# Delta attention and two MoE layers on one core: MoE from chunk 0's first tokens, packed diagonal blocks, VectorE transposes, another order of weight loads

## The chip, the cores and the metric

One core of a Trainium2 chip runs the whole program. Its engines are TensorE (PE, with its weight loads PEld), VectorE (DVE), ScalarE (ACT), GpSimd (POOL) and SyncE (SP, which issues most transfers); each works through its own instructions in order and waits on semaphores of the others. The metric is the device time of one execution in microseconds (us).

## The reference

```python
B, H, S, D = 4, 8, 768, 48                      # float32
k_n = k / (norm(k) + 1e-6); state = zeros((B, H, D, D))
for t in range(S):
    y[:, :, t] = q_t @ state                    # per head
    v_old = state^T @ k_n_t
    state = state + beta_t * outer(k_n_t, v_t - v_old)
x = y.transpose(0, 2, 1, 3).reshape(3072, 384)
x = maximum(x @ w_in, 0) ** 2 @ w_out           # d_ff 2048, weights float64
g = x @ w_gate
out = (g * sigmoid(g) * (x @ w_val)) @ w_out2   # d_ff 1536, weights float64
```

## The kernel before

The sequence is cut into six chunks J of 128 steps, each in two halves c of 64. With all four batches a chunk gives 512 tokens (TOK; HT is 256, the tokens of one c). Of the 32 pairs of batch and head, p picks 16 partitions' worth of heads, and each tile of 128 partitions holds two blocks of 64.

For a chunk, attention solves a triangular system per head: the Gram blocks of the keys (`gram`, `gram0`), masked and scaled by beta, are inverted and merged into NT. Chunk 0 inverts 16x16 blocks on DVE (`invert16`) and merges them twice on PE: `d_merge1` and `d_merge2` to 32x32, `tr11`, `merge1`, `merge2` to 64x64. The other chunks send their masked Gram (`m_out`) to memory, load it in another layout (`t_load`), invert 32x32 blocks on POOL (`invert`), and fetch the result (`n_out`, `n_back`). Then per half c come the correction by the state (`ks`), the solution u (`uu`), the output y (`y0` for chunk 0, straight into MoE's input xh and xl; `yy` for the others, through memory, `fetch_x` and `split_x`) and the state (`do_ku`). c=1 needs the state of c=0.

The first MoE layer runs chunk by chunk over 16 steps m of 128 hidden features: `moe1_h` (nine matmuls to ps_h), ACT's Relu and squares, DVE's low part hl, `moe1_o` (nine into ps_y, held in PSUM over all m). Products are split in a high and a low fp32r part. HMS[J] says how many of the first m run on half the tokens, c by c. The weights are float64 words of 16 pieces of 768 columns, w_in and w_out in turn, two m each. `Piece` turns a piece into its two parts: ACT's Abs into f, three DVE operations (lines 180, 182, 187), ACT's high part (200), and the low part (203) on DVE or POOL, as `conv_lo` says. The converted pieces are then kept for all chunks. The second MoE layer follows at the end and is not touched.

The order on DVE, ACT, POOL, PE and SP is that of the code where `manual_schedule` names the engine. Ahead of the MoE loop it is written out by hand (lines 1124 to 1227). In the loop, a list `first` (and `plan` for later chunks) gives a time slot to each attention stage: a full m step is two slots, a half one is one. `conv_slot` and `need` bring the conversions along. Chunk J+1's MoE waits for its x. In the kernel before, all of chunk 0's attention stands ahead of the first MoE matmul, and the list starts with chunk 1's scores.

Of the kernel before, what the change touches and what calls it, by code (L numbers as in the profile page):

```python
# [21 lines left out]
def delta_attention_moe_moe2_kernel(  # L22
# [186 lines left out]
    raw1 = {  # L209
        (pc, kd): wp.tile([128, Z * PIECE], WDT, tag="w", name="raw")  # L210
        for pc in range(NP1 - 2) for kd in range(2)
    }
# [255 lines left out]
    def m0(J, c, p):
        m, ps = MS[J, c, p], g0.pop((J, c, p))
        for d, r in parts(p):  # L470
            nc.vector.scalar_tensor_tensor(out=m[d], in0=ps[r], scalar=-1.0, in1=m[d], op0=ALU.mult, op1=ALU.mult)


# [204 lines left out]
    def tr11(J, c):  # L678
        ts = [
            TD[0][:, p] if J == 0 and c else ap.tile([128, 8, 32], F32, tag="tq", bufs=2, name="tq") for p in range(2)  # L680
        ]
        if J == 0:
            pss = banks([128, 8, 32], "ps_tq")
            for h in range(8):
                for p in range(2):
                    for b0 in (0, 64):
                        nc.tensor.matmul(
# [716 lines left out]
```

## Time and profile before

| what | us |
|---|---|
| median of 3 runs (1082.63 to 1083.14) | 1083.07 |
| the profiled execution, its own time | 1081.49 |
| its span, first to last instruction | 1079.6 |
| PE busy | 995.8 (92%) |
| DVE busy | 610.7 (57%) |
| ACT busy | 398.4 (37%) |
| POOL busy | 249.5 (23%) |

The shares are means over stages with different limits, so they are read by stretches. In the page's 40 slices of 27 us PE has 3, 3, 6, 7, 6, 7, 8 and 8 tenths in the first eight and 9 in nearly all others; DVE has 6 to 8 there.

### The profile page before, as it was taken

To read this page: it belongs to the slowest core of one execution; us is meant where nothing else is said; L and a number is where in the kernel's file an instruction comes from. 1 tells how busy PE (TensorE), PEld (TensorE's weight loads), DVE (VectorE), ACT (ScalarE), POOL (GpSimd) and SP (SyncE) were. 2 spreads that over 40 slices of the span, in tenths; PEclk is the share of its full clock that TensorE was granted. 3 is DMA by queue.
4 is the path that set the end of the run, shared out by engine and by line. 5 is a ranking of instruction groups with operands and counts; after the bars stand their busy time and mean duration, and the time that the engine had idled before them with its cause. 6 is when DMAs were issued, how large, how long until landed. Compare 5 with 4: busy or idle time off the path is not lost.

```text
span 1079.6 us, 24471 instructions
## 1 busy us (share of the span) xinstructions
PE 995.8 (92%) x10591; PEld 816.5 (76%) x10591; DVE 610.7 (57%) x979; ACT 398.4 (37%) x765; POOL 249.5 (23%) x373
## 2 busy tenths in 40 slices
PE   3367678899999999999999999999999999999998
PEld 3355556688887787787788878888888888888886
DVE  6647888778567667754546995343343343433333
ACT  6243545542353344344347873132231222312222
POOL 3629417914811940950000000000000000000000
PEclk9998888989999999999999999999999999999999
DMA  9474044526235253231015660010010100100000
GB/s 301 174 195 126 2 104 109 138 77 149 66 101 122 68 132 73 59 99 42 20 30 197 193 240 13 1 59 1 1 59 1 53 7 1 59 1 1 30 0 30
DMA packets 118267, 84.51 MB, mean 78 GB/s; under 512 B 91664, under 2 KB 95632, under 8 KB 118160
## 3 DMA queue, kind: packets, MB, share of 16 engines
q1 hardware_dynamic: 116960, 77.97, 26.1%
q0 software_dynamic: 1056, 4.72, 1.1%
q8 instruction: 83, 1.36, 0.5%
q10 hardware_dynamic: 144, 0.26, 0.1%
q14 instruction: 24, 0.20, 0.1%
HBM read 61.70 MB, written 21.23 MB: 77 GB/s over the span
## 4 chain that ended last, share of the span: by engine, by line
PE 68%; issue 9%; DMA 5%; DVE 4%; ACT 2%; POOL 1%; SPq 1%; ACTq 0%; DVEq 0%; POOLq 0%
PE ps_o L1083 14%; PE ps_v L1058 13%; PE ps_g L1058 13%; PE ps_h L957 11%; PE ps_y L991 11%; DMA raw<-in_moe_w_gate_dram 1%; PE ps_y L784 1%; DVE raw L182 1%; PE ps_k L732 1%; PE ps_g L431 1%; DVE w L203 1%; PE ps_u L747 1%; PE ps_a L541 1%; DMA x2raw<-y_scr 1%; DMA y_scr<-ye 1%
## 5 line engine op out<-in xcount | busy, mean ns | idle before, releaser
L957 PE MATMUL ps_h<-xh,w 128*128 128x512 f32 (+1 forms) x636 | 206.8, 385 | 12.9 <-DVE w L203 12.8
L991 PE MATMUL ps_y<-hh,w 128*128 128x512 f32 (+1 forms) x606 | 157.4, 394 | 10.0 <-DVE w L203 4.7
L957 PEld LDWEIGHTS ps_h<-xh,w 128*128 128x128 f32 x636 | 119.0, 193 | 37.5 <-DVE w L203 14.6
L1062 DVE SCALAR_TENSOR_TENSOR th<-th,ps_g 128x512 f32<-128x512 f32 x72 | 49.5, 687 | 170.6 <-ACT th L1061 170.5
L1058 PE MATMUL ps_g<-x2h,w 128*128 128x512 f32 x432 | 144.8, 389 | 0.0
L1058 PE MATMUL ps_v<-x2h,w 128*128 128x512 f32 x432 | 144.7, 389 | 0.0
L960 ACT ACTIVATE r<-ps_h 128x512 f32<-128x512 f32 (+1 forms) x106 | 58.9, 556 | 218.2 <-PE ps_h L957 213.9
L991 PEld LDWEIGHTS ps_y<-hh,w 128*128 128x128 f32 x606 | 109.6, 192 | 33.0 <-DVE w L203 5.6
L957 PE MATMUL ps_h<-xl,w 128*128 128x512 f32 (+1 forms) x318 | 120.1, 378 | 0.0
L590 POOL TENSOR_TENSOR TMP<-T 128x30 f32<-128x30 f32 (+9 forms) x150 | 92.2, 615 | 111.7 <-DMA T<-m_scr 69.0
L1083 PE MATMUL ps_o<-ph,w 128*128 128x512 f32 x432 | 111.9, 389 | 1.4 <-ACT ye L1007 1.4
L1061 ACT ACTIVATE th<-ps_g 128x512 f32<-128x512 f32 x72 | 43.1, 599 | 180.2 <-PE ps_g L1058 180.2
L597 POOL TENSOR_TENSOR T<-T,TMP 128x30 f32<-128x30 f32 (+9 forms) x150 | 95.2, 635 | 11.0
L1083 PEld LDWEIGHTS ps_o<-ph,w 128*128 128x128 f32 x432 | 81.0, 188 | 18.6 <-ACT ye L1007 1.9
L1065 ACT ACTIVATE ph<-th 128x512 fp32r<-128x512 f32 x72 | 45.4, 631 | 133.1 <-DVE th L1063 133.1
L1058 PEld LDWEIGHTS ps_g<-x2h,w 128*128 128x128 f32 x432 | 81.1, 188 | 17.1 <-issue 0.3
L1058 PEld LDWEIGHTS ps_v<-x2h,w 128*128 128x128 f32 x432 | 81.1, 188 | 16.8
L991 PE MATMUL ps_y<-hl,w 128*128 128x512 f32 (+1 forms) x303 | 84.0, 386 | 1.5 <-DVE hl L977 1.5
L976 DVE TENSOR_TENSOR r<-r 128x512 f32<-128x512 f32 (+1 forms) x72 | 50.2, 697 | 62.0 <-ACT hh L961 61.5
L1058 PE MATMUL ps_v<-x2l,w 128*128 128x512 f32 x216 | 84.0, 389 | 0.0
L1058 PE MATMUL ps_g<-x2l,w 128*128 128x512 f32 x216 | 84.0, 389 | 0.0
L977 DVE TENSOR_TENSOR hl<-r,hh 128x512 fp32r<-128x512 f32 (+1 forms) x106 | 74.6, 705 | 12.7 <-ACT r L964 8.0
(137 smaller groups left out, 1384.2 us busy)
## 6 DMA issues: line engine op xcount, KB each, us to landing
raw<-in_moe_w_out_dram SPq DMA_DIRECT2D x13, 768.0 KB, 5.2
raw<-in_moe_w_in_dram SPq DMA_DIRECT2D x8, 768.0 KB, 11.4
KT<-in_kt_dram SPq DMA_DIRECT2D x12, 448.0 KB, 6.4
m_scr<-M SPq DMA_DIRECT2D x20, 256.0 KB, 2.4
KB<-in_kn_dram SPq DMA_DIRECT2D x12, 384.0 KB, 6.0
AQ<-in_q_dram SPq DMA_DIRECT2D x24, 192.0 KB, 4.9
V<-in_v_dram SPq DMA_DIRECT2D x12, 384.0 KB, 3.9
raw<-in_moe_w_gate_dram SPq DMA_DIRECT2D x6, 768.0 KB, 4.4
```

The source lines that it names most:

```text
L590: eng.tensor_tensor(tmp[:, r0:r1], t_[:, r0:r1, kk:kk + 1].to_broadcast([n, r1 - r0, w]), t_[:, kk:kk + 1, kk + 1:].to_broadcast([n, r1 - ...
L597: eng.tensor_tensor(t_[:, r0:r1, kk + 1:], t_[:, r0:r1, kk + 1:], tmp[:, r0:r1], op=ALU.add)
L957: nc.tensor.matmul(ps, w_[:, kk], x_[:, kk, cols], start=n == 0, stop=n == 3 * KD - 1)
L960: nc.scalar.activation(out=r, in_=ps, func=ACTF.Relu)
L976: nc.vector.tensor_tensor(r, r, r, op=ALU.mult)
L977: nc.vector.tensor_tensor(hl, r, hh.bitcast(F32), op=ALU.subtract)
L991: nc.tensor.matmul(acc[f], w_[:, fs], h_, start=first, stop=m == NM1 - 1 and n == 2)
L1058: nc.tensor.matmul(ps, w_[:, kk], x_[:, kk], start=n == 0, stop=n == 3 * KD - 1)
L1061: nc.scalar.activation(out=th, in_=gp, func=ACTF.Tanh, scale=0.5)
L1062: nc.vector.scalar_tensor_tensor(out=th, in0=th, scalar=1.0, in1=gp, op0=ALU.add, op1=ALU.mult)
L1065: nc.scalar.activation(out=hh, in_=th, func=ACTF.Copy)
L1083: nc.tensor.matmul(o_acc[J][f], w_[:, fs], h_, start=m == 0 and n == 0, stop=m == NM2 - 1 and n == 2)
```

## The change

Ahead of the loop, chunk 0's diagonal 32x32 blocks go from PSUM into a packed tile DG (`g_diag`) before they are transposed, all 128 partitions in one transpose; the other Gram blocks follow (`g_off`). Chunk 1's Gram is copied by ACT (`m_copy`) and masked and scaled by POOL (`m_mask`, `m_beta`). `tr11` transposes on DVE instead of by matmuls with the identity. The scores of chunk 0's c=1 and of chunk 1 are copied by ACT and masked by POOL instead of masked by DVE. Only the first half of chunk 0 is finished ahead of the loop; the c=1 half's stages move into `first`. HMS goes to 6 for chunk 0 and 2 for chunk 1, chunk 2's slots four later. Three weight pieces are asked for at the start, the others one by one between other transfers. The first two low parts go to POOL.

```diff
-    HMS = [0, 1, 1, 1, 1, 1]
-    LAGS = [0] * 6
+    HMS = [6, 2, 1, 1, 1, 1]
+    LAGS = [0, 0, 4, 0, 0, 0]
...
-                if turn[0] and not last_in:
+                if turn[0] and not last_in and not held:
...
-    conv_lo = [nc.vector]
+    conv_lo = [nc.gpsimd]
...
+    def g_diag(c, p):
+        ps = g0[0, c, p]
+        for b0 in range(0, 128, 32):
+            r0, f0 = ps_row(p, b0), b0 % 64
+            out_, in_ = DG[b0:b0 + 32, 16 * c + 8 * p:16 * c + 8 * p + 8], ps[r0:r0 + 32, :, f0:f0 + 32]
+            if p == 0:
+                copy(out_, in_)
+            else:
+                nc.vector.tensor_copy(out_, in_)
...
+    def m_copy(J, c, p):
...
+        for d, r in parts(p):
+            nc.scalar.activation(out=m[d], in_=ps[r], func=ACTF.Copy, scale=-1.0)
+
+    def m_mask(J, c, p):
+        m = MS[J, c, p]
+        nc.gpsimd.tensor_tensor(m, m, mask.unsqueeze(1).to_broadcast([128, 8, 64]), op=ALU.mult)
...
-        nc.gpsimd.tensor_tensor(BM, BM, bT.unsqueeze(1).to_broadcast([128, 32, 32]), op=ALU.mult)
+        nc.vector.tensor_tensor(T, T, bT.unsqueeze(1).to_broadcast([128, 32, 32]), op=ALU.mult)
...
-        for b0 in range(0, 128, 32):
-            f0 = b0 % 64
-            nc.vector.transpose(
-                out=T[b0:b0 + 32], in_=NTT[b0:b0 + 32, :, f0:f0 + 32].rearrange("s x t -> s t x")
-            )
+        nc.vector.transpose(out=T, in_=DG.rearrange("s x t -> s t x"))
...
-                            ident[b0:b0 + 32, b0:b0 + 32], start=True, stop=True,
...
+            src = NT[c][p][:, :, 0:32] if J else ND[:, 16 * c + 8 * p:16 * c + 8 * p + 8]
+            nc.vector.transpose(out=t11[c, p], in_=src)
...
-    for pc, kd in ((1, 0), (1, 1), (2, 0), (2, 1), (3, 0), (3, 1), (4, 0)):
-        load_w1(pc, kd)
...
+    load_w1(1, 0)
+    make_identity(nc, ident)
...
+    stage("y", 0, 0)
     run_all(("tload", 1, c) for c in P2)
     run(("v", 1, 0))
     run(("mback", 1, 0))
     run(("ku", 0, 0))
+    held.clear()
+    merge16("d1", 1)
+    run(("vn", 0, 1))
+    conv(2)
+    flush()
+    run(("inv", 1, 0, 1, nc.gpsimd))
...
-            8: [("gram", 2, 0)],
-            10: [("gram", 2, 1), ("loadw", 7, 0)],
-            13: [("nout", 1), ("nback", 1, 0), ("nback", 1, 1), ("vn", 1, 1)],
...
+            0: [("d2", 1, 0), ("d2", 1, 1)],
+            0.5: [("ks", 0, 1)],
+            1: [("t11", 0, 1), ("m1", 0, 1), ("dcopy", 1)],
...
+            15: [("gram", 2, 1), ("loadw", 7, 0)],
...
+            16.5: [("nout", 1), ("nback", 1, 0), ("tload", 2, 0), ("tload", 2, 1), ("nback", 1, 1)],
```

PE around chunk 0's u of c=0. ps_d and ps_e are the merges to 32x32, ps_tq the transposes by identity, ps_m and ps_x the merges to 64x64, ps_u is u, ps_y is y, ps_s the state. Before:

```order
L653 MATMUL ps_d<-own,ND 32x16 x64
L687 MATMUL ps_tq<-own,ND 32x32 x32
L671 MATMUL ps_e<-ND,own 32x16 x64
L704 MATMUL ps_m<-tq,NT 32x32 x32
L687 MATMUL ps_tq<-own,ND 32x32 x32
L719 MATMUL ps_x<-ND,tq 32x32 x32
L747 MATMUL ps_u<-V,NT 64x48 x32
L704 MATMUL ps_m<-ND,NT 32x32 x32
```

Now, from the first merge of c=0 on:

```order
L665 MATMUL ps_d<-NDT,ND 32x16 x64
L683 MATMUL ps_e<-ND 32x16 x64
L701 MATMUL ps_m<-tq,NT 32x32 x32
L716 MATMUL ps_x<-ND,tq 32x32 x32
L744 MATMUL ps_u<-V,NT 64x48 x32
L814 MATMUL ps_y<-AQ_100,RS_103 32x64 x32
L814 MATMUL ps_y<-AQ_100,RS_104 32x64 x32
```

The second half's merges (ps_d, ps_tq, ps_e of c=1) stood between c=0's steps; now u of c=0 follows its own merges, and y comes directly behind it.

DVE behind the scaling of that u (RS is the tile of u and the state). f and raw rows are conversion steps, xl the low part of MoE's input, hl that of a MoE block, V the correction of c=1 by the state. Before:

```order
L753 TENSOR_TENSOR RS0_103<-ps_u_972,bB_98 64x8x48 x2
L753 TENSOR_TENSOR RS1_104<-ps_u_973,bB_98 64x8x48 x2
L560 TENSOR_TENSOR AQ1_101<-ps_a_1132,mask_96 64x512 x2
L560 TENSOR_TENSOR AQ1_101<-ps_a_1133,mask_96 64x512 x2
L740 TENSOR_TENSOR V_163<-V_163,ps_k_1239 128x384
L740 TENSOR_TENSOR V_163<-V_163,ps_k_1240 64x384 x2
L203 TENSOR_TENSOR w1_827<-raw_116,w1_827 128x6x128
L187 SCALAR_TENSOR_TENSOR raw_117<-raw_117 128x768
```

Now:

```order
L834 TENSOR_TENSOR xl_868<-ps_y_833,xh_867 128x3x64
L834 TENSOR_TENSOR xl_868<-ps_y_834,xh_867 128x3x64
L834 TENSOR_TENSOR xl_868<-ps_y_873,xh_867 128x3x64
L834 TENSOR_TENSOR xl_868<-ps_y_874,xh_867 128x3x64
L179 TENSOR_SCALAR f_831<-f_831 128x768
L181 SCALAR_TENSOR_TENSOR raw_157<-raw_157,f_831 128x768
L974 TENSOR_TENSOR hl_1104<-r_1102,hh_1103 128x256
L974 TENSOR_TENSOR hl_1121<-r_1119,hh_1120 128x256
L737 TENSOR_TENSOR V_155<-V_155,ps_k_1218 128x384
L737 TENSOR_TENSOR V_155<-V_155,ps_k_1219 64x384 x2
L186 SCALAR_TENSOR_TENSOR raw_157<-raw_157 128x768
L202 TENSOR_TENSOR w1_1256<-raw_157,w1_1256 128x6x128
```

The low parts hl of the first two half blocks and the conversion steps now stand ahead of c=1's correction, which before had come first.

SP from the first values on. V are values, raw weight pieces, M the masked Gram of chunk 1 on its way out and T its way back, AQ, KB and KT the next queries and keys. Before:

```order
L325 DMA V_163<-in_v_dram 128x768
L141 DMA raw_118<-in_moe_w_in_dram 128x3x512
L141 DMA raw_119<-in_moe_w_out_dram 128x2x768
L141 DMA raw_120<-in_moe_w_in_dram 128x3x512
L141 DMA raw_121<-in_moe_w_out_dram 128x2x768
L141 DMA raw_122<-in_moe_w_in_dram 128x3x512
L141 DMA raw_123<-in_moe_w_out_dram 128x2x768
L141 DMA raw_124<-in_moe_w_in_dram 128x3x512
L527 DMA m_scr1_90<-M_712 128x8x64
L527 DMA m_scr1_90<-M_714 128x8x64
L527 DMA m_scr1_90<-M_874 128x8x64
```

Now:

```order
L321 DMA V_155<-in_v_dram 128x768
L139 DMA raw_157<-in_moe_w_in_dram 128x3x512
L539 DMA m_scr1_90<-M_442 128x8x64
L539 DMA m_scr1_90<-M_444 128x8x64
L539 DMA m_scr1_90<-M_451 128x8x64
L539 DMA m_scr1_90<-M_453 128x8x64
L544 DMA T_109<-m_scr1_90 32x32x32 x4
L321 DMA V_915<-in_v_dram 128x768
L642 DMA NT_102<-m_scr1_90 32x16x32 x2
L139 DMA raw_1090<-in_moe_w_out_dram 128x2x768
L139 DMA raw_1092<-in_moe_w_in_dram 128x3x512
L317 DMA AQ0_100<-in_q_dram 48x2x512 x2
```

Nine pieces were asked for ahead of the stores of M; now three are, and the fourth comes behind the stores, the loads of T and chunk 1's values.

## Rows read from the trace of the kernel before

**Rows 1.** Stage table of core 0: busy us (instructions) per engine, granted clock, DMA share, GB/s.

```profile
0.00:87.00 87.00, 42.16 (x1854) 38.40 (x1856) 53.55 (x126) 35.34 (x127) 41.64 (x58) 0.98 0.72 214
87.00:150.00 63.00, 42.14 (x457) 31.25 (x446) 47.95 (x69) 25.57 (x39) 32.32 (x46) 0.81 0.21 59
150.00:219.00 69.00, 59.94 (x1006) 47.37 (x1005) 58.54 (x81) 39.05 (x72) 49.50 (x67) 0.92 0.51 126
219.00:630.00 411.00, 407.44 (x5340) 332.61 (x5339) 272.81 (x457) 184.48 (x350) 123.93 (x199) 1.00 0.38 101
630.00:1080.00 450.00, 444.10 (x1956) 366.83 (x1956) 177.82 (x251) 113.92 (x178) 2.15 (x4) 1.00 0.08 27
```

**Rows 2.** Timeline of DVE: start us, us, operation, count, idle before and releaser.

```profile
14.44 7.79 DVE L487 STREAM_TRANSPOSE T<-NT 32x1024 f32<-32x1024 f32 x4
...
33.71 1.88 DVE L494 STREAM_TRANSPOSE own<-T 128x1024 f32<-128x1024 f32 x1
...
71.62 2.81 DVE L560 TENSOR_TENSOR AQ<-ps_a,mask 64x512 f32<-64x512 f32 x4 [9.12 <-PE ps_a L541]
```

**Rows 3.** Timeline of ACT, start of the program.

```profile
13.06 2.40 ACT L567 ACTIVATE AQ<-ps_a 64x512 f32<-64x512 f32 x4 [0.89 <-PE ps_a L541]
...
36.84 0.37 ACT L655 ACTIVATE ND<-ps_d,lower 128x128 f32<-128x128 f32 x1 [10.03 <-PE ps_d L653]
...
47.20 1.54 ACT L676 ACTIVATE tq<-ps_tq 32x256 f32<-32x256 f32 x4 [2.19 <-PE ps_tq L687]
```

**Rows 4.** Timeline of PE: one stop, and the first MoE matmul.

```profile
39.38 1.51 PE L671 MATMUL ps_e<-ND 32*32 32x16 f32 x98 [1.33 <-issue]
...
87.14 0.50 PE L957 MATMUL ps_h<-xh,w 128*128 128x512 f32 x1
```

**Rows 5.** Groups by line and shape, 0 to 220 us: count | busy us, mean ns | idle.

```profile
L187 DVE SCALAR_TENSOR_TENSOR raw<-raw 128x768 int32<-128x768 int32 x15 | 18.2, 1210 | 0.2
...
L182 DVE SCALAR_TENSOR_TENSOR raw<-raw,f 128x768 int32<-128x768 int32 x15 | 16.2, 1078 | 0.4
...
L203 DVE TENSOR_TENSOR w<-raw,w 128x768 fp32r<-128x768 f32 x11 | 13.2, 1201 | 0.1
L977 DVE TENSOR_TENSOR hl<-r,hh 128x512 fp32r<-128x512 f32 x15 | 13.0, 869 | 2.8 <-ACT r L964 2.8
...
L560 DVE TENSOR_TENSOR AQ<-ps_a,mask 64x512 f32<-64x512 f32 x16 | 11.0, 688 | 12.1 <-PE ps_a L541 11.8
...
L180 DVE TENSOR_SCALAR f<-f 128x768 int32<-128x768 int32 x15 | 10.6, 705 | 17.1 <-ACT f L174 16.9
...
L203 POOL TENSOR_TENSOR w<-raw,w 128x768 fp32r<-128x768 f32 x4 | 8.3, 2065 | 35.9 <-ACT w L200 35.9
...
L370 ACT ACTIVATE junk<-KB 128x48 f32<-128x48 f32 x32 | 7.2, 229 | 3.0 <-DMA KB<-in_kn_dram 3.0
```

**Rows 6.** Timeline of SP's DMA issues from 150 us.

```profile
150.07 0.36 SPq L527 DMA_DIRECT2D m_scr<-M  x1
...
151.40 0.43 SPq L624 DMA_DIRECT2D n_scr<-T  x1
...
161.56 2.62 SPq L532 DMA_DIRECT2D T<-m_scr  x4
...
218.17 0.33 SPq L624 DMA_DIRECT2D n_scr<-T  x1
```

**Rows 7.** Timeline of POOL: first and last operation of chunk 2's inverse.

```profile
168.92 0.25 POOL L590 TENSOR_TENSOR TMP<-T 128x30 f32<-128x30 f32 x1 [5.90 <-DMA T<-m_scr]
...
217.91 0.24 POOL L597 TENSOR_TENSOR T<-T,TMP 128x30 f32<-128x30 f32 x1
```

**Rows 8.** Chain of work that ended last, 222 to 232 us: start us, us, what.

```profile
223.46 1.07 PE ps_h L957 x9
...
225.61 2.07 PE ps_h L957 x9
...
230.82 0.68 PE ps_m L704 x50
```

More of the change, by code (lines that the diff above doesn't have):

```diff
@@ L150, in delta_attention_moe_moe2_kernel @@
     last_in = []
+    held = [1]
     class Piece:
@@ L208, in delta_attention_moe_moe2_kernel @@
     LAST = (NP1 - 1, 1)
[L209 to L212, printed above, removed]
+    raw1 = {}
     conv1 = [(pc, kd, 0) for pc in range(NP1) for kd in range(2)] + [(*LAST, 1)]
@@ L468, in m0, with ps_row @@
[L468 to L471, printed above, removed]
+    def ps_row(p, b0):
+        return (b0 + 64 * p) % 128
+    def g_diag(c, p):
[7 more added lines that the diff above has]
+                nc.vector.tensor_copy(out_, in_)
@@ new lines, in g_off @@
+    def g_off(c, p):
+        ps = g0.pop((0, c, p))
+        for b0 in (0, 64):
+            r0 = ps_row(p, b0)
+            nc.scalar.activation(
+                out=NT[c][p][b0:b0 + 32, :, 32:64], in_=ps[r0:r0 + 32, :, 32:64], func=ACTF.Copy, scale=-1.0
+            )
+    def m_copy(J, c, p):
+        if J == 1 and c:
+            m = ap.tile([128, PIECE], F32, tag="xf", bufs=2, name="M")[:, 0:512].rearrange("q (h t) -> q h t", h=8)
+        else:
+            m = ap.tile([128, 8, 64], F32, tag="xr", bufs=XR, name="M")
+        MS[J, c, p], ps = m, g0.pop((J, c, p))
+        for d, r in parts(p):
+            nc.scalar.activation(out=m[d], in_=ps[r], func=ACTF.Copy, scale=-1.0)
@@ L678, in tr11 @@
     def tr11(J, c):
[L679 to L687, printed above, removed]
[L688 to L697 removed]
+        for p in range(2):
+            t11[c, p] = ap.tile([128, 8, 32], F32, tag="tq", bufs=2, name="tq")
+            src = NT[c][p][:, :, 0:32] if J else ND[:, 16 * c + 8 * p:16 * c + 8 * p + 8]
+            nc.vector.transpose(out=t11[c, p], in_=src)
     def merge1(J, c):
@@ L1122, in merge16 @@
         run_all((w, c, p) for p in P2)
-    run_all(("kt", 0, c) for c in P2)
-    nc.sync.dma_start(out=bB, in_=beta)
-    run_all(("kb", 0, c) for c in P2)
-    nc.gpsimd.memset(BM, 1.0)
+    nc.gpsimd.memset(NTT, 0.0)
+    nc.gpsimd.memset(BM, -1.0)
     nc.gpsimd.affine_select(
@@ L1148, in delta_attention_moe_moe2_kernel @@
         )
-    make_identity(nc, ident)
     for p in P2:
@@ L1158, in delta_attention_moe_moe2_kernel @@
     run(("brows",))
-    run(("din",))
-    run(("amm", 0, 0))
     run_all(("gram0", 1, c) for c in P2)
+    for c in P2:
+        run_all(("go", c, p) for p in P2)
+    run(("sums", 1, 0))
+    run_all(("amm", 0, c) for c in P2)
+    stage("mcopy", 1, 0)
+    run(("sq", 1, 1, 0))
+    stage("mcopy", 1, 1)
     run(("acopy", 0))
-    run_all(("sums", 1, c) for c in P2)
-    run(("root", 1, None, 0))
+    run(("acopy", 1))
     ahead()
@@ L1297, in delta_attention_moe_moe2_kernel @@
                 load_last()
-            conv_lo[0] = nc.gpsimd if n in range(5, 8) else nc.vector
+            if n and J and not seq[n - 1][0]:
+                order.close()
+                order.enter_context(tc.manual_schedule(engines={mybir.EngineType.DVE, mybir.EngineType.Activation}))
             nxt = seq[n + 1] if n + 1 < len(seq) else None
```

186 lines of the change are left out of this document (81 added, 105 removed).

## The prediction

> **What bounds the kernel now.** I read the stage table first [rows 1]. From 219 us on, TensorE (PE) is busy all but 9.5 us of 861, at full clock; nothing the change does can shorten that part except by starting it earlier. [...] So the question is when the kernel gets to that dense part. The first MoE matmul stands at 87.14 [rows 4]. From there to 219 VectorE (DVE) is the busiest: 47.95 of 63 and 58.54 of 69 us. It turns each float64 weight piece into fp32r parts by four operations, 0.71 + 1.08 + 1.21 + 1.20 = 4.2 us [rows 5], seventeen times, and its idle times are waits for PE or ScalarE (ACT), such as the 9.12 us ahead of 71.62 [rows 2].
>
> A second chain runs through the queue of SyncE (SP) and GpSimd (POOL). The last masked Gram block of chunk 2 leaves for memory at 150.07, queued ahead of chunk 1's inverse (issued 151.40); then chunk 2's blocks come back (loads from 161.56), POOL inverts them from 168.92 to 218.15, and the result leaves at 218.17 [rows 6, 7]. PE uses it at 230.82 [rows 8]. I call the 150.07 T: chunk 1's merge and chunk 2's inverse both hang on it. From T to 230.82 are 80.7 us.
>
> **The front, step by step.** The diagonal blocks were transposed 32 partitions at a time, 7.79 us [rows 2]; packed in DG they need one transpose of the size of line 494, 1.88. The packing is eight 32x256 copies on DVE, a form it does not show; ACT's takes 0.385 (1.54 for four) and DVE's 64x512 mask 0.688 [rows 3, 5]; I take 0.40, by ACT's row of the same shape. With 5 us for the norms' root, now behind the transpose, and the 13.4 us that run from the end of line 487 to the end of line 494, NDT is ready at about 6.9 + 3.2 + 1.9 + 5 + 1.4 (the new multiply by beta, 1024 columns at the mask's rate) + 13.4 = 31.8 instead of 35.6.
>
> ACT is level with that. Ahead of the first merge copies its order now holds eight copies (3.1), sixteen sums (half of the 7.2 for 32), six Gram copies (3.6 at 0.60 [rows 3]), eight score copies (4.8) and three operations of 384 to 768 columns (1.8): 16.9 us after a root at about 15.8, so 32.7, when PE's first product, a microsecond behind NDT, is there too; before, these copies started at 36.84, so 4 us are won. Should ACT's order run late, the chain runs late with it, since nothing hides it. From there: copies and second merge of c=0 to 37.3 (one stop of PE within, below), the two transposes of 128x256 (a quarter of 1.88, 0.47 each) to 38.3, first merge product 39.2, ACT held by an Abs until 40.4 and copying to 41.9, second product, a high part and four copies to 44.4, u to 45.6, its DVE scaling to 47.8. The transposing PE products (two blocks of 32), chunk 0's c=1 merge and its second state are no longer ahead of MoE. y, the state and c=1's first merge are 160 products in one go. PE stops for 1.33 us ahead of 39.38 with no releaser but "issue", and does so after every 128 of the small matmul records [rows 4]; I allow two stops of 2 us beside 3 us of work. First MoE matmul: about **55**, 32 us earlier. If the packing copies cost 0.69, 2 us later; without the stops, 4 earlier.
>
> [...]
>
> **How much of the 32 us lasts.** MoE now runs six m steps on 256 tokens, with weights as they come, then the same six on the other half. A half block costs PE 1.07 against 2.07 us [rows 8], so halving is nearly free. But the pieces come at DVE's pace, so I count DVE's work up to T, in the new order. Before: 53.55 + 47.95 = 101.5 us busy of 150 [rows 1], 48.5 idle. Taken away: transposes 5.9, two Gram copies (at 0.69) 1.4, twelve score masks 8.3 (chunk 0's c=1 and chunk 1 now go ACT and POOL), six Gram masks 4.1, three subtractions that fall behind T 1.6; together 21.3. Added: packing 3.2, beta 1.4, more conversion steps 9.1 (3 x 0.71 + 2 x 1.08 + 3 x 1.21 + 1.20; two low parts go to POOL), two sums 1.0, two copies 1.2, four transposes 1.9, and twelve half-width low parts for three full ones, 12 x 0.47 - 3 x 0.87 = 3.0 (0.47: a little over half of 0.87); together 20.8. So DVE has **101.0** us to do before T, as before: T moves only by the idle time that the order fills. Waits that I can name there: the first Gram 7, ACT's root 1.5, u 2, the first y 3, the first two half blocks 5, the correction by the state 3, u, y and state of c=1 7: 28.5. I add 10.5 for couplings through ACT's order (a piece's Abs or high part queued behind a MoE block that waits for DVE). T = 101 + 39 = **140**. Bounds: named waits alone, 130; all the old idle time back and a fifth more of it, 159.
>
> Behind T: the inverse's way out and chunk 2's way in took 18.85 us (150.07 to 168.92); four instead of eight return transfers stand between, 2 less: 16.8. POOL's 49.2 us held two low parts of 2.07 [rows 5] and waits for DVE; without them 43.5 to 45. Out, back and transposed, 9. Together 69 to 71, against 80.7. PE's own work from T to the same point comes to about as much: chunk 1's first merge T + 11, then 54 us of blocks, and 5 of stops at low clock. I take 71, so chunk 2's first merge product starts at 211 instead of 230.8. By then PE has also done more of chunk 1's MoE: four half steps and two and a half full ones against two halves and two h blocks, 8.4 us by [rows 8]. What is left is thus 8.4 shorter.
>
> **Sum.** 230.8 - 211 + 8.4 = 28.2; less 1 because chunk 2's slots come four later (LAGS), which uses up most of the slack of chunk 3's inverse. So 27 us off the profiled execution's 1081.49 (span 1079.6), 1054.5; it lies 1.6 below the median 1083.07, so the median goes to **1056**.
>
> **Rivals.**
> DVE keeps up fully: T = 130 and 69 behind it give 1083 - (239.2 - 199) = 1043. For it speaks that POOL's first inverse now ends near 98, leaving DVE alone for the later pieces; against it, all couplings must vanish. 0.16.
>
> Little of the idle time is won: T = 150 to 159 and 73 behind it, 1067 to 1076. For it: PE idles cold between blocks (0.81 now), and the inverse, from about 54, lies on the pieces that MoE waits for first. Line 187 takes 1.21 in the mean. [...] 0.20.
>
> Slower: SP's queue starves the conversion. Nine weight pieces were asked for by 26 us; now three are, and the other thirteen stand in SP's order behind stores of M, transfers that wait for PE's y and state of c=1, and other loads. If ten pieces each come so late that 3 us show, T = 172 and the end is 1083 + 172 + 71 - 239.2 = 1087; it decides once T passes 168. Against: in the estimate the first held piece is asked for at 54 and wanted at 70. 0.11.
>
> No change: T near 167, by a mixture of these, 0.04. Also the first half steps could wait for POOL's low parts (behind chunk 1's Gram work, to 53), which moves MoE's start and little else.
>
> **Numbers.** Forecast 1056 with 0.49 (1048 to 1066 by itself). Range 1042 to 1076, leaving out the slower case, no change, and a few hundredths below. A change under 0.2% (2.2 us) cannot be told from none: faster 0.85, within 0.04, slower 0.11.
>
> **What would show it.** First MoE matmul between 51 and 59; line 487's successor one transpose of 1.9; the first merge copies near 33; DVE's busy share up to T above 0.68; T (the fourth store of chunk 2's M) near 140; a POOL inverse of 43 to 45 behind it; PE dense from about 195. It is wrong if T stays at 150, or if PE stops in chunk 1's MoE for chunk 2's inverse for more than a few us.

## The result, and the profile after

The changed kernel takes 1087.88 us (median; 1087.19 to 1090.30), beside 1082.77 for the kernel before on the same chip. The ratio is 1.0056 (95% interval 1.0039 to 1.0073): slower by about 6 us, where 27 us less was forecast. The profiled executions differ by a little more, spans of 1088.3 against 1079.6, since the profiled one was the slowest of the five after.

The stage table of the kernel after, with the windows of [rows 1]: busy us (instructions) of PE, PEld, DVE, ACT and POOL, the granted clock, the DMA share and GB/s.

```profile
0.00:87.00 87.00, 36.84 (x1371) 33.33 (x1371) 52.04 (x120) 38.52 (x108) 55.40 (x74) 0.70 0.61 171
87.00:150.00 63.00, 47.29 (x727) 42.41 (x728) 41.83 (x65) 36.98 (x72) 24.76 (x33) 0.82 0.27 92
150.00:219.00 69.00, 61.16 (x1080) 48.54 (x1078) 55.53 (x83) 38.27 (x71) 37.22 (x57) 0.93 0.53 130
219.00:630.00 411.00, 400.36 (x5427) 326.87 (x5426) 261.15 (x439) 177.15 (x342) 127.75 (x208) 0.99 0.37 98
630.00:1088.00 458.00, 451.88 (x1990) 372.99 (x1988) 185.75 (x260) 121.50 (x187) 2.16 (x4) 1.00 0.09 32
```

Beside [rows 1] PE was busy 5.3 us less in the first 87 us, though MoE is among it now; it made up 5.2 in the next 63 and 1.2 in the next 69, and has 8.0 us more idle time behind 219 (4.96 of it one stop across 219 to 224; the kernel before had a stop of 4.86, in another place of PE's order, just ahead of 219). Over the whole span PE is idle 90.8 us against 83.8 and busy 997.5 against 995.8: 7.0 and 1.7 make up the 8.7 between the spans. That sum, PE's idle time plus its busy time, is the account I use below. PE's work is nearly fixed, so the end moves mostly with PE's stops; but its busy time goes from 992.3 to 1001.5 us in the table below, and part of two losses lies there.

The first of them is the wait for the first merge, before 16.09 us, now 16.51 and five us later. The timeline of PE (start us, us, operation, count, idle before and its releaser), with the first MoE matmul at 69.70:

```profile
40.94 1.43 PE L665 MATMUL ps_d<-NDT,ND 16*32 16x16 f32 x91 [16.51 <-DVE NDT L502]
...
69.01 0.77 PE L665 MATMUL ps_d<-NDT,ND 16*32 16x16 f32 x41 [3.84 <-issue]
69.70 0.58 PE L954 MATMUL ps_h<-xh,w 128*128 128x256 f32 x1
...
77.67 1.04 PE L683 MATMUL ps_e<-ND,NDT 32*32 32x16 f32 x59 [3.63 <-issue]
...
85.24 0.32 PE L729 MATMUL ps_k<-RS,KT 48*64 48x48 f32 x4 [2.44 <-issue]
88.70 0.58 PE L954 MATMUL ps_h<-xh,w 128*128 128x256 f32 x1 [3.14 <-ACT w L199]
```

Why the merge is late stands in the timelines of DVE and of POOL (GpSimd) between 10 and 41 us. The one transpose is there as forecast (1.90), and so is the packing (3.45 for eight). But the 16x16 inverse behind them, a row of short DVE operations, has long ones among it:

```profile
10.41 1.90 DVE L497 STREAM_TRANSPOSE T<-own 128x1024 f32<-128x1024 f32 x1
...
21.18 1.98 DVE L622 TENSOR_TENSOR TMP<-T 128x36 f32<-128x36 f32 x2
23.09 0.33 DVE L631 TENSOR_TENSOR T<-T,TMP 128x36 f32<-128x36 f32 x2
23.34 0.38 DVE L622 TENSOR_TENSOR TMP<-T 128x44 f32<-128x44 f32 x2
23.63 2.53 DVE L631 TENSOR_TENSOR T<-T,TMP 128x44 f32<-128x44 f32 x2
...
38.94 1.85 DVE L502 STREAM_TRANSPOSE NDT<-T 128x1024 f32<-128x1024 f32 x1
```

```profile
21.07 1.93 POOL L507 TENSOR_TENSOR NT<-NT,bB 128x1024 f32<-128x1024 f32 x1
23.54 5.13 POOL L479 TENSOR_TENSOR M<-M,mask 128x512 f32<-128x512 f32 x4 [0.55 <-ACT M L475]
29.23 2.39 POOL L585 TENSOR_SCALAR_AFFINE_SELECT AQ<-AQ 64x1024 f32<-64x1024 f32 x2 [0.56 <-ACT AQ L579]
31.71 1.48 POOL L326 TENSOR_TENSOR V<-V,nB 128x768 f32<-128x768 f32 x1
```

A pair of the same shape (128x36) takes 0.33 or 1.98, and each long operation lies beside a GpSimd operation of about its length. The inverse runs from 19.91 to 37.08, 17.2 us; before it took 8.1 (23.77 to 31.86). In the kernel before GpSimd was kept away: line 1171 copied one element per partition of the inverse's result to a tile `mark`, in GpSimd's order ahead of all this work, so that it waited for the inverse. The timelines of DVE and of POOL of the kernel before:

```profile
25.04 0.30 DVE L610 TENSOR_TENSOR TMP<-T 128x36 f32<-128x36 f32 x2
```

```profile
31.98 0.19 POOL L1171 COPY mark<-T 128x1 f32<-128x1 f32 x1 [7.03 <-DVE T L621]
```

The change drops that line, adds the masks (479, 585), and puts them ahead of the inverse's end. The diff in this document leaves the line out; I had read past it.

T, the last store of chunk 2's masked Gram, moved from 150.07 [rows 6] to 164.13:

```profile
164.13 0.36 SPq L539 DMA_DIRECT2D m_scr<-M  x1
164.59 0.53 SPq L139 DMA_DIRECT2D raw<-in_moe_w_in_dram  x1
165.21 0.49 SPq L636 DMA_DIRECT2D n_scr<-T  x1
```

### The profile page after: what moved, and what is told of

It is laid out like the page before. It is cut to its first block, busy times and chain, and to the rows that moved or that the text cites. A ratio compares the mean times of both kernels' runs of the same rounds, so it can differ in the third digit from the quotient of the medians.

```text
span 1088.3 us, 24484 instructions
## 1 busy us (share of the span) xinstructions
PE 997.5 (92%) x10589; PEld 824.1 (76%) x10589; DVE 596.3 (55%) x963; ACT 412.4 (38%) x779; POOL 247.3 (23%) x374
## 3 DMA queue, kind: packets, MB, share of 16 engines
q0 software_dynamic: 1056, 4.72, 1.1%
q8 instruction: 83, 1.36, 0.5%
## 4 chain that ended last, share of the span: by engine, by line
PE 68%; issue 11%; DVE 8%; DMA 5%; ACT 4%; POOL 3%; SPq 0%; DVEq 0%; ACTq 0%; POOLq 0%
PE ps_o L1080 13%; PE ps_v L1055 13%; PE ps_g L1055 13%; PE ps_h L954 11%; PE ps_y L988 10%; DVE raw L181 1%; POOL TMP L602 1%; DMA raw<-in_moe_w_out_dram 1%; POOL T L609 1%; DMA raw<-in_moe_w_gate_dram 1%; PE ps_y L781 1%; PE ps_u L744 1%; DVE w L202 1%; PE ps_g L427 1%; DVE T L631 1%
## 5 line engine op out<-in xcount | busy, mean ns | idle before, releaser
L954 PE MATMUL ps_h<-xh,w 128*128 128x512 f32 (+1 forms) x678 | 213.5, 377 | 8.8 <-ACT w L199 5.3
L954 PEld LDWEIGHTS ps_h<-xh,w 128*128 128x128 f32 x678 | 128.4, 198 | 31.0 <-ACT w L199 5.8
L1059 DVE SCALAR_TENSOR_TENSOR th<-th,ps_g 128x512 f32<-128x512 f32 x72 | 49.5, 688 | 170.5 <-ACT th L1058 170.4
L988 PEld LDWEIGHTS ps_y<-hh,w 128*128 128x128 f32 x648 | 113.5, 194 | 37.4 <-ACT w L199 8.2
L954 PE MATMUL ps_h<-xl,w 128*128 128x512 f32 (+1 forms) x339 | 125.1, 369 | 0.0
L602 POOL TENSOR_TENSOR TMP<-T 128x30 f32<-128x30 f32 (+9 forms) x150 | 88.4, 589 | 142.9 <-DMA T<-m_scr 100.1
L609 POOL TENSOR_TENSOR T<-T,TMP 128x30 f32<-128x30 f32 (+9 forms) x150 | 92.3, 616 | 11.3
L1055 PEld LDWEIGHTS ps_g<-x2h,w 128*128 128x128 f32 x432 | 81.1, 188 | 17.2 <-ACT hh L958 0.4
L1055 PEld LDWEIGHTS ps_v<-x2h,w 128*128 128x128 f32 x432 | 81.1, 188 | 16.8
```

The costliest lines, as they stand in the source:

```text
L602: eng.tensor_tensor(tmp[:, r0:r1], t_[:, r0:r1, kk:kk + 1].to_broadcast([n, r1 - r0, w]), t_[:, kk:kk + 1, kk + 1:].to_broadcast([n, r1 - ...
L609: eng.tensor_tensor(t_[:, r0:r1, kk + 1:], t_[:, r0:r1, kk + 1:], tmp[:, r0:r1], op=ALU.add)
L954: nc.tensor.matmul(ps, w_[:, kk], x_[:, kk, cols], start=n == 0, stop=n == 3 * KD - 1)
L988: nc.tensor.matmul(acc[f], w_[:, fs], h_, start=first, stop=m == NM1 - 1 and n == 2)
L1055: nc.tensor.matmul(ps, w_[:, kk], x_[:, kk], start=n == 0, stop=n == 3 * KD - 1)
L1059: nc.vector.scalar_tensor_tensor(out=th, in0=th, scalar=1.0, in1=gp, op0=ALU.add, op1=ALU.mult)
```

## The experiments

Twelve kernels were run. The table puts them together. Ratio: time against the kernel before on the same chip, with its interval. Merge: start of PE's first merge product. MoE: first MoE matmul. Idle and busy are PE's, from the profiled execution (span less busy).

| kernel | median us | ratio | merge | MoE | T | idle | busy |
|---|---|---|---|---|---|---|---|
| before | 1082.8 | 1 | 35.7 | 87.1 | 150.1 | 83.8 | 995.8 |
| changed | 1087.9 | 1.0056 (1.0039 to 1.0073) | 40.9 | 69.7 | 164.1 | 90.8 | 997.5 |
| nomark | 1085.5 | 1.0038 (1.0025 to 1.0050) | 38.7 | 92.3 | 154.7 | 87.9 | 995.4 |
| guard | 1079.8 | 0.9981 (0.9970 to 0.9992) | 32.2 | 61.6 | 155.4 | 81.2 | 996.6 |
| early | 1083.6 | 1.0012 (0.9999 to 1.0024) | 40.7 | 67.8 | 157.1 | 84.7 | 995.9 |
| conv3 | 1093.3 | 1.0102 (1.0086 to 1.0119) | 41.0 | 68.1 | 161.2 | 90.5 | 1001.0 |
| guard_early | 1075.5 | 0.9945 (0.9929 to 0.9961) | 31.7 | 60.7 | 150.5 | 76.4 | 996.7 |
| nout9 | 1072.8 | 0.9916 (0.9903 to 0.9930) | 31.7 | 61.3 | 149.9 | 75.5 | 995.6 |
| shift3 | 1082.6 | 0.9999 (0.9985 to 1.0012) | 31.9 | 61.8 | 145.1 | 78.3 | 1001.5 |
| whole | 1069.1 | 0.9880 (0.9862 to 0.9898) | 31.6 | 89.5 | 134.9 | 75.6 | 992.3 |
| whole_late | 1090.2 | 1.0077 (1.0059 to 1.0095) | 31.8 | 89.5 | 157.1 | 88.1 | 997.8 |
| whole_late2 | 1075.7 | 0.9941 (0.9928 to 0.9953) | 31.9 | 88.4 | 146.4 | 79.8 | 994.0 |
| whole_nout | 1066.8 | 0.9857 (0.9836 to 0.9879) | 31.7 | 89.0 | 134.7 | 71.1 | 993.6 |
| whole_fill | 1072.6 | 0.9919 (0.9902 to 0.9937) | 31.8 | 92.6 | 138.9 | 75.7 | 994.8 |

### GpSimd beside the inverse: guard and nomark

My theory was that GpSimd's operations, now beside the inverse, stretch it; the rivals were that the loss lies later, and that the operations are slow for another reason. `guard` puts the wait back into the changed kernel:

```diff
-    run(("drest",))
-    stage("mmask", 1, 0)
-    stage("mmask", 1, 1)
-    run(("asel", 0))
     run(("inv0", range(14, 0, -1)))
+    nc.gpsimd.tensor_copy(mark, T[:, 0, 0:1])
+    run(("drest",))
+    stage("mmask", 1, 0)
+    stage("mmask", 1, 1)
+    run(("asel", 0))
```

> The changed kernel with one row put back from the kernel before: GpSimd's one-element copy that reads the inverse's result stands again ahead of GpSimd's masks, so that these run behind the 16x16 inverse instead of beside it. Theory A (GpSimd beside DVE's short operations stretches the inverse, 17.2 us after against 8.1 before): the inverse falls to 8.0 to 8.5 us, NDT is ready near 32, the first merge product starts near 32 instead of 40.9, the first MoE matmul near 61 instead of 69.7, and the end comes 6 to 9 us earlier than the changed kernel's 1087.9, so 1079 to 1082. [...] Rival C (GpSimd has nothing to do with it, the operations are slow for their data): the inverse stays at 17.

`nomark` does the opposite to the kernel before: it takes that one line away.

```diff
     run(("inv0", range(14, 0, -1)))
-    nc.gpsimd.tensor_copy(mark, T[:, 0, 0:1])
     run(("dout",))
```

> The kernel before without GpSimd's one-element copy that made it wait for the inverse. Two memsets of 1.9, a product of 1.9, a product of 1.5 us and mask products of 5.7 us may then run beside DVE's inverse. Theory A: the inverse grows from 8.1 to 14 to 17 us and the first merge is as much later; if the front sets the end one to one, 1089 to 1092; if DVE's conversion hides it, 1083 to 1086. Rival C: inverse stays at 8.1, time within 1 us of 1082.8.

With the wait back, the inverse takes 8.1 us again (20.11 to 28.24). The timelines of PE and POOL of `guard`:

```profile
32.18 1.43 PE L665 MATMUL ps_d<-NDT,ND 16*32 16x16 f32 x91 [6.99 <-DVE NDT L502]
```

```profile
28.36 0.19 POOL L1172 COPY mark<-T 128x1 f32<-128x1 f32 x1 [7.06 <-DVE T L633]
28.50 1.91 POOL L507 TENSOR_TENSOR NT<-NT,bB 128x1024 f32<-128x1024 f32 x1
30.37 4.96 POOL L479 TENSOR_TENSOR M<-M,mask 128x512 f32<-128x512 f32 x4
35.28 2.36 POOL L585 TENSOR_SCALAR_AFFINE_SELECT AQ<-AQ 64x1024 f32<-64x1024 f32 x2
```

The merge comes 8.8 us earlier, T 8.8, the median 8.1: what the front gains goes to the end nearly whole, and the wait costs GpSimd nothing, since in the changed kernel it stood idle from 33 to 49 anyway.

In `nomark` the loss was smaller than I expected (3.0 us at the merge, 3.2 at the end), and its rows say why. Timelines of DVE and of POOL:

```profile
26.69 0.40 DVE L610 TENSOR_TENSOR TMP<-T 128x54 f32<-128x54 f32 x2
27.00 2.09 DVE L619 TENSOR_TENSOR T<-T,TMP 128x54 f32<-128x54 f32 x2
28.98 1.71 DVE L610 TENSOR_TENSOR TMP<-T 128x56 f32<-128x56 f32 x2
```

```profile
25.00 1.93 POOL L499 MEMSET NT<- 32x1024 f32 x2
27.00 1.98 POOL L501 TENSOR_TENSOR NT<-NT,bB 128x1024 f32<-128x1024 f32 x1
28.95 1.47 POOL L330 TENSOR_TENSOR V<-V,nB 128x768 f32<-128x768 f32 x1
```

Beside the two memsets (25.00 to 26.93) DVE kept its pace; beside the two products one operation each waited them out. I had counted the memsets and the mask products of 5.7 us as well, but those need `bB`, which DVE makes behind the inverse.

The traces of `nomark` and of the changed kernel agree in each point: beside the two products (1.98 and 1.47 us) a pair of DVE operations took 2.09 and 1.71, and beside line 585's two selections (2.39 us together) 1.34 and 1.36, where pairs of those shapes took 0.39 to 0.43 with GpSimd idle; beside the memsets, which read nothing, they took 0.31 to 0.40.

### The load order, and the sum: early and guard_early

`early` asks for five more pieces at the start and drops the calls that asked for them from 65 us on:

```diff
-    load_w1(1, 0)
+    for pc, kd in ((1, 0), (1, 1), (2, 0), (2, 1), (3, 0), (3, 1)):
+        load_w1(pc, kd)
```

> The changed kernel with five of the later weight loads asked for at the start again, directly behind the third, instead of one by one from 65 us on. If the rush of transfers from 64 to 80 us (DMA share 0.99) is what stretches PE's three stops there (3.84, 3.63 and 2.44 us, against 1.2 to 2.0 ahead of it): they fall to about 2 each, the first MoE matmul comes 2 us earlier, and T, the last store of chunk 2's M, 4 to 5 us earlier; the end at 1083 to 1084. If the conversion was starved by SP's queue, as my rival had it: T falls by more than 10 us and the end to below 1080. If the stops do not depend on the transfers: end within 1 us of 1087.9. If early loads only move the rush under chunk 0's own inputs and stops: 1088 or more.

Between 64 and 87 us PE's stops were 3.84, 3.63 and 2.44 in the changed kernel. With the loads early the timeline of PE has

```profile
67.15 0.77 PE L665 MATMUL ps_d<-NDT,ND 16*32 16x16 f32 x41 [3.02 <-issue]
67.84 0.58 PE L954 MATMUL ps_h<-xh,w 128*128 128x256 f32 x1
...
75.98 0.32 PE L729 MATMUL ps_k<-RS,KT 48*64 48x48 f32 x4 [0.38 <-issue]
```

and none of over 1 us between these: 9.9 us of stops became 3.4. T is 7.0 us earlier, more than the 4 to 5 expected, the end 4.3. So the loads asked for "one by one between other transfers" were no spread: nothing was asked for between 18 and 55 us, and then five pieces and the next inputs came in a heap (DMA share 0.91 from 64 to 87 us, in `early` 0.38). But no conversion step of the changed kernel waited for a piece of weights; starving was not what the heap did. The length of the stops goes with the transfers beside them. Of all stops of PE of 1.2 us or more up to 110 us that name no releaser but "issue", in the fourteen traces, the 26 with a DMA share of 0.06 or less beside them took 1.33 to 2.31 us; every longer one, up to 4.77 in `whole_fill`, had a share of 0.25 or more, though short ones stand there too. In `whole`, below, they are 3.57 and 4.11 us, at shares of 0.99 and 0.55. No run takes the transfers alone away, so that they cause the length is not shown.

`guard_early` has both edits.

> Both repairs at once: GpSimd's masks behind the inverse, and five weight loads asked for at the start. Each by itself gave 8.1 and 4.3 us. If they act at two places of one chain (the inverse up to 41 us, the stops at 65 to 87): they add up, T (the last store of chunk 2's M) near 148 to 150, PE's last long stop, ahead of chunk 1's MoE, ends 60 us behind T at 208 to 210, and the end is 863 us behind that: 1073 to 1076 as a median. If both only fed the same slack, or the early loads now collide with GpSimd's and PE's earlier front: 1079 to 1081.

1075.5, as the sum of the two gains (8.1 + 4.3) says. The stop ahead of chunk 1's MoE ended at 210.2, and the span 862.9 behind it, as in the runs before (864.1 in the changed kernel, 862.5 in `guard`, 863.3 in `early`). So two mistakes of order cost 12.4 us, and the change without them is worth 0.55% against the kernel before. The early loads may have a price of their own: PE's first stop, with no transfer beside it in `guard`, has a DMA share of 0.57 beside it in `guard_early`. The timeline of PE, of `guard` and then of `guard_early`:

```profile
35.37 0.67 PE L665 MATMUL ps_d<-NDT,ND 16*32 16x16 f32 x35 [1.76 <-issue]
```

```profile
37.05 0.67 PE L665 MATMUL ps_d<-NDT,ND 16*32 16x16 f32 x35 [3.94 <-issue]
```

### Moving a conversion step forward: conv3

DVE stood 7.7 us twice between 65 and 86 us, once for ACT and once for PE, with the third step of the third piece behind it in its order.

```diff
     run(("vn", 0, 1))
-    conv(2)
+    conv(3)
     flush()
```

> The changed kernel with one conversion step more ahead of MoE: the third step of the third piece stands on DVE ahead of the first low parts and of the correction V, not behind them. In the changed kernel it ran at 86.75, behind two waits of 7.7 us for PE, and PE waited 3.14 us for its weights at 88.70. If these waits in DVE's order set T: the step runs near 66, PE's wait at 88.7 goes, every later piece comes 3 us or more earlier, the end at 1083 to 1085. If DVE's total of work up to T sets it, or another wait takes its place: end within 1 us of 1087.9.

T came 2.9 us earlier, as expected, and the end 5.5 later: the theory fell. With every later step one place ahead, the Abs of the last piece (line 173), which in the changed kernel ran behind the copies of chunk 1's merge to NT (184.23 behind 182.64), now stands ahead of them on ACT, and waits there for its transfer, issued at 177.22. The timeline of ACT, and PE's u behind it:

```profile
181.44 0.54 ACT L173 ACTIVATE f<-raw 128x384 f32<-128x384 f32 x1 [5.04 <-DMA raw<-in_moe_w_out_dram]
182.01 0.60 ACT L957 ACTIVATE r<-ps_h 128x512 f32<-128x512 f32 x1
...
183.84 1.55 ACT L688 ACTIVATE NT<-ps_x 32x256 f32<-32x256 f32 x4
```

```profile
184.29 3.08 PE L744 MATMUL ps_u<-V,NT 64*64 64x48 f32 x64 [3.31 <-POOL TMP L602]
```

The row names GpSimd as the releaser of u; GpSimd's inverse is not an input of it, and the first copy of NT at 183.84 is what it was waiting for. This wait is not shown to be the whole loss: over the profiled executions (the changed kernel's was its slowest) PE's idle time is the same, 90.5 against 90.8, and it is the busy time that is 3.5 us longer, 1001.0 against 997.5, for which no run has a cause.

### Chunk 1's inverse sent out early: nout9

In the changed kernel GpSimd has chunk 1's inverse at 108 and SP sends it at 165.21. `nout9` is `guard_early` with

```diff
-            9: [("sq", 2, 0, 1), ("sq", 2, 1, 0)],
+            9: [("nout", 1), ("nback", 1, 0), ("nback", 1, 1), ("sq", 2, 0, 1), ("sq", 2, 1, 0)],
...
-            16.5: [("nout", 1), ("nback", 1, 0), ("tload", 2, 0), ("tload", 2, 1), ("nback", 1, 1)],
+            16.5: [("tload", 2, 0), ("tload", 2, 1)],
```

> The two repairs, and chunk 1's inverse is sent out and fetched at slot 9 instead of 16.5, ahead of the stores of chunk 2's M in SP's queue. GpSimd has it ready at 108 in the changed kernel, where it left at 165. Theory D (behind T it is chunk 1's own way that sets the end, 60 us from T to the end of PE's stop ahead of its MoE): the wait for NT ahead of chunk 1's first merge (4.9 us in the run with GpSimd's guard alone) goes, and the end is 3 to 6 us earlier than with the two repairs alone. Rival (my prediction's view: conversions, and the way of chunk 2's inverse, set it): within 1 us of the two repairs alone.

2.7 us faster than `guard_early` (0.29%, the two intervals just touch), a little below what was expected. PE's wait ahead of chunk 1's first merge fell from 3.44 to 1.57, the stop ahead of its MoE from 4.82 to 4.12. So chunk 1's own way is on the path, and I had let it run along with chunk 2's inverse.

### Half the tokens first, or all: whole, whole_late, whole_late2, shift3

The change's first item is that MoE begins with half of chunk 0's tokens. `whole` takes that away from `guard_early` and keeps the rest:

```diff
-    HMS = [6, 2, 1, 1, 1, 1]
+    HMS = [0, 2, 1, 1, 1, 1]
...
     run(("loadk", 2, 0))
+    merge16("d2", 1)
+    ahead()
+    run(("ks", 0, 1))
+    conv(2)
...
-            0: [("d2", 1, 0), ("d2", 1, 1)],
-            0.5: [("ks", 0, 1)],
...
-            15: [("gram", 2, 1), ("loadw", 7, 0)],
...
+            10: [("gram", 2, 1), ("loadw", 7, 0)],
```

> The two repairs, but MoE begins with all of chunk 0's tokens: the stages of its second half stand ahead of the loop, HMS[0] is 0 again, the slots five earlier. This takes away the part of the change that its title names first, and keeps the packing, the DVE transposes and ACT's and GpSimd's share of the masks. If beginning with half the tokens is worth what the prediction gave it (first MoE matmul 30 us earlier, most of it kept): the first MoE matmul near 80, T 15 us later or more, 1088 or more. If the pieces' conversion on DVE sets the pace whatever PE has to multiply: T within 5 us of the two repairs alone and the time within 4 us of theirs. If half blocks at the lower clock and their extra copies cost more than they give: faster than the two repairs alone.

It is 6.3 us faster than `guard_early`, with MoE beginning 29 us later. But two things are undone at once, the halves and the five slots that chunk 0's second half took (the weight loads move with the slots). `whole_late` puts the slots back, `shift3` moves them three ahead with the halves kept.

> The run that begins MoE with all of chunk 0's tokens (1069.1 against 1075.5 with half of them) also had all later stages five slots earlier, so that chunk 2's Gram stands beside MoE's steps 4 and 5 instead of 6 and 7. Here it begins with all tokens and the slots stay where the changed kernel has them. If beginning with half the tokens is what cost the 6 us: within 2 us of 1069. If the slots did it (T has fewer pieces to convert ahead of it): 1075 or more, T near 155.

> The other half of that question: the two repairs, MoE begins with half the tokens as in the changed kernel, and all stages behind chunk 0's stand three slots earlier. If the slots set T: T falls from 150 to 143 or less and the end to 1070 to 1072. If beginning with half the tokens sets it (DVE's conversion steps wait behind the low parts and corrections of the half blocks): T moves by less than 3 us, PE waits for weights as before, and the end stays within 2 us of 1075.5.

`whole_late` lost 21 us against `whole`, but for a reason of its own. ACT's timeline has three Abs that wait for weights, which whole blocks want sooner:

```profile
150.18 0.89 ACT L173 ACTIVATE f<-raw 128x768 f32<-128x768 f32 x1 [11.35 <-DMA raw<-in_moe_w_out_dram]
163.09 0.89 ACT L173 ACTIVATE f<-raw 128x768 f32<-128x768 f32 x1 [9.39 <-DMA raw<-in_moe_w_in_dram]
176.29 0.55 ACT L173 ACTIVATE f<-raw 128x384 f32<-128x384 f32 x1 [5.50 <-DMA raw<-in_moe_w_out_dram]
```

`shift3` brought T to 145.1, 5.4 earlier, and lost at the end: 0.54% by the ratios, some 6 us (7.1 between the medians, which are of two chips). PE then stood 6.09 us for chunk 1's inverse ahead of its merge, and was busy 4.8 us longer for the same work; what made it busy longer is not shown. T alone doesn't set the end. So `whole_late2`: whole blocks, late slots, and only the loads five slots earlier.

```diff
+            9.99: [("loadw", 7, 0)],
...
-            15: [("gram", 2, 1), ("loadw", 7, 0)],
...
+            15: [("gram", 2, 1)],
```

> The run with all tokens first and the later stages at the changed kernel's slots (1090.2) was short of weights: ACT stood 11.4, 9.4 and 5.5 us for pieces that were still on their way, since MoE by whole blocks wants them twice as fast and the loads stood at the same slots. Here the loads alone are five slots earlier, the stages stay late. If the shortage of weights was the whole loss: within 2 us of 1069, so that beginning with half the tokens costs some 6 us against it wherever the stages stand. If late stages are bad for whole blocks: 1074 to 1080, and the two orders are about equal at these slots. If the shortage was not it: 1085 or more.

1075.7 against 1075.5: with the stages at the same slots, no difference can be measured between MoE beginning with half the tokens at 61 us and with all of them at 88. One piece of weights was still late, the last, which SP issued at 158.65, behind chunk 1's inverse on its way out and back and chunk 2's blocks. The timelines of ACT and of PE of `whole_late2`:

```profile
162.82 0.55 ACT L173 ACTIVATE f<-raw 128x384 f32<-128x384 f32 x1 [8.04 <-DMA raw<-in_moe_w_out_dram]
```

```profile
165.56 2.26 PE L716 MATMUL ps_x<-NT,tq 32*32 32x32 f32 x64 [6.28 <-ACT tq L688]
```

ACT's copies for chunk 1's merge stand behind that Abs, and PE stood 6.28 us for them. So the two orders are about equal with this wait in one of them; with the last piece in time, all tokens first could be up to 6 us the faster, which no run here tests. That the early start gains nothing holds either way. The stage tables of `guard_early` and of `whole_late2`, the first two windows each, show where 28 us of earlier start go:

```profile
0.00:87.00 87.00, 46.17 (x1535) 41.40 (x1535) 54.38 (x133) 47.74 (x127) 61.69 (x79) 0.72 0.58 172
87.00:150.00 63.00, 49.48 (x731) 42.99 (x730) 46.19 (x70) 36.56 (x66) 21.58 (x31) 0.87 0.36 117
```

```profile
0.00:87.00 87.00, 42.43 (x1646) 37.66 (x1650) 53.82 (x132) 44.40 (x117) 61.03 (x79) 0.84 0.59 172
87.00:150.00 63.00, 53.83 (x602) 41.85 (x592) 60.61 (x79) 40.96 (x63) 28.75 (x31) 0.97 0.46 142
```

Up to 87 us DVE did the same, 54.4 and 53.8: an earlier MoE brings hardly a piece of weights sooner. PE was busy 3.7 us longer there with the halves. In the next window DVE did 46.2 with the halves and 60.6 without, and PE gave the gain back (49.5 against 53.8). The order of DVE's steps offers a reason, that with halves they stand behind low parts and corrections that wait for PE and ACT; no run takes that alone. Over the whole span the halves have 3.4 us less idle time of PE and 2.7 us more busy time. The granted clock in the two windows is 0.72 and 0.87 against 0.84 and 0.97, but it doesn't account for the busy time: `shift3`, with the halves too, has 0.93 up to 87 us and is as long busy there, 46.30 against 46.17.

`whole` is 0.61%, some 6.6 us, faster than `whole_late2`. How much of that the earlier slots give is open, since the wait of 6.28 us for the last piece lies in the difference.

### The fastest: whole_nout, and one step too far, whole_fill

In `whole` PE stood 6.32 us ahead of chunk 1's merge:

```profile
147.54 1.43 PE L701 MATMUL ps_m<-tq,NT 32*32 32x32 f32 x64 [6.32 <-issue]
```

`whole_nout` sends the inverse out at slot 7 instead of 11.5, with the edit of `nout9`.

> All of chunk 0's tokens first, and chunk 1's inverse sent out and fetched at slot 7 instead of 11.5. In the run without this PE stood 6.3 us ahead of chunk 1's first merge, with the inverse's way out and back in its queue behind T (135). If this wait is on the path: it goes, and the end is 4 to 6 us earlier, 1063 to 1065. If the merge then waits for something else, or the 2.9 us stop ahead of chunk 1's MoE grows by as much: within 2 us of 1069.

The stop is gone, and 4.5 us of PE's idle time in the profiled execution, but the medians, of two chips, differ by only 2.3 and the intervals of the two ratios overlap: it is no slower, and how much faster stays open. At 0.9857 of the kernel before (0.9836 to 0.9879), 1066.8 us, it is the fastest of all. `whole_fill` then moves conversion steps into the 11 us that DVE stands idle from 59 to 70:

```diff
     run(("vn", 0, 1))
-    conv(2)
+    conv(3)
+    ahead()
+    conv(3)
     flush()
```

> The fastest so far (all tokens first, chunk 1's inverse sent early, 1066.8), with four conversion steps and a low part more on DVE ahead of the correction V of chunk 0's second half, where DVE stood 12 us for PE (58 to 70) while raw pieces lay ready. If DVE's total up to T sets T: T falls by 5 us or more, the later waits for DVE's low parts (3.9 and 2.9 us) go, 1061 to 1064. If, as when one step was moved in the changed kernel, what the step brings forward stands in front of something else in ACT's order (its Abs waits, and the copies behind it): 1066 or more.

It lost 0.62%, the second time that moving steps forward did. DVE's transposes for c=1's merge start at 75.91 instead of 73.71, PE's u at 83.02 instead of 80.08, and MoE at 92.55 instead of 88.96: the steps now stand ahead of the chain that MoE waits for.

## Why the prediction was wrong

The forecast was 1056, the result 1087.9. In the terms of the prediction's sum, most of these 31.9 us are four steps: 8.1 the length of the inverse in the front, 4.3 the load order, which it put at nothing, 10.5 DVE's idle time up to T (T at 150.5 in `guard_early` instead of 140), and 8.5 PE's own work behind T (79.5 us there instead of 71).

**The front.** Packing, one transpose and the order behind them came about as worked out. The step that failed here is "the 13.4 us that run from the end of line 487 to the end of line 494", carried over as if nothing could change it. Another engine's work had been kept from running beside it, and the change let it: the inverse in that stretch took 17.2 us instead of 8.1. In a rival I had set POOL's later inverse beside the conversion steps, where the trace of the kernel before shows a cost (line 187 took 1.40 and 1.35 us beside chunk 1's inverse, at 93.76 and 102.59, and 0.95 with POOL idle, at 123.94 and 132.89), and not asked what else of POOL's now lies beside a DVE chain. With the wait back the first merge product starts at 32.2; I had NDT at 31.8. The price was 8.1 us of the result.

**The first MoE matmul.** Forecast 55, measured 69.7, and 60.7 in `guard_early`. Of the last 5.7, 3.6 are PE's two stops in c=0's merges in `guard_early`: 3.94 and 1.70, where I had counted one of 2. The two behind u were 0.89 and 2.75, within the 4 that I allowed there. But the products beside them (y, the state, c=1's first merge), "3 us of work", took 6.1 (PE's busy time from 50.50 to 60.72). The forecast has no term for the load order, and it was worth 4.3 us. Nor do the stops need transfers beside them: every trace has one of 1.7 us or more with a DMA share of 0.06 or less beside it (2.22 us in the kernel before, 2.02 in the changed one). What PE waits for in them no run shows.

**How much lasts.** The work was right: 101.0 us of DVE up to T forecast, 101.07 measured in `guard_early` (up to 150.5; 107.67 up to 164.13 in the changed kernel, with the inverse's waits in it). The idle time was not: the sum 101 + 39 took 39 for the 48.5 of before, and it was 49.4 in `guard_early`. I listed the waits I could name and added an allowance of 10.5; taking the named 28.5 as they stand, what is left is 20.9, twice the allowance. That it comes from DVE's steps being spread between MoE's low parts and attention's corrections is read from the order, not shown. Without GpSimd's and the loads' share this is the rival "little of the idle time is won" (T of 150 to 159, 1067 to 1076): 150.5 and 1075.5. I gave it 0.20.

**Behind T.** In the changed kernel the inverse's way to GpSimd took 16.1 us (16.8 forecast) and the inverse 40.9 (43.5 to 45): that arm of the sum held. The other didn't, PE's own work, "chunk 1's first merge T + 11, then 54 us of blocks, and 5 of stops". The merge came at T + 11.1, but behind it PE was busy 62.3 us and stood 6.3, so that chunk 2's first merge product followed 79.7 behind T, not 71, with PE busy without a stop in the last 19.6 us ahead of it. [rows 1] could have told: from 150 to 219 PE was busy 59.94 us and DVE, which the prediction calls the busiest there, 58.54. What PE stood for was chunk 1's merge (3.58) and ACT's copies behind chunk 1's x (4.96), which I had only counted as running along.

**The rivals.** The time of the result, 1087.9, is that of the slower rival (1087), but not by its mechanism: T stayed below its point of 168, and no conversion step waited for a weight piece. Where weights do come late, in `whole_late`, the mechanism is real and costs 14.5 us (against `whole_late2`). The range ended below the result, because it held no case in which the front itself gets later.

**What stays open.** Whether earlier slots help whole blocks, and why they harm half blocks, is argued from the rows (the late piece in `whole_late2`, the merge wait in `shift3`), not shown by a run that takes one cause alone. What sets the length of PE's stops without a releaser (0.4 to 4.8 us) was not isolated either: `early` shows that the load order changes their sum, and the long ones have transfers beside them in every trace.

## What to carry to other kernels

Before a chain of short operations is carried over at its old length, list what the change puts beside it on other engines (here GpSimd beside VectorE); a line that seems to do nothing may be there to keep them apart. An earlier start of the bound engine is worth only what its feeder brings sooner: compare the feeder's work up to that point (here 54 us of DVE up to 87 us either way) before counting the start as a gain. And steps moved forward in an engine's order can delay the chain that stands behind them, on that engine and on the next (in `whole_fill` DVE's transposes by 2.2 us, PE's u by 2.9, MoE by 3.6).

## What the runs showed of the hardware

In the changed kernel short DVE operations with two inputs from SBUF took about as long as the GpSimd operation that read SBUF beside them: a pair that took 0.31 us in `guard`, with GpSimd idle, took 1.98 beside line 507's 1.93, and the inverse went from 8.1 to 17.2 us. Beside the two GpSimd memsets in `nomark` (1.93 us together) such pairs took 0.31 to 0.40. And PE's stops in runs of small matmuls, up to 110 us of the fourteen traces, took at most 2.31 us where the DMA share beside them was 0.06 or less, and up to 4.77 where it was 0.25 or more. I had taken 2 us as their size, though the trace of the kernel before has stops of 3.51 and 2.99 among them (ahead of 70.24 and 81.10).
